# Where the operands of TensorE lie in SBUF: an attention and two MLP layers on one core

## The chip, the core and the metric

The kernel runs on one core of a Trainium2 chip. A core has engines that work side by side, each through its own list of instructions in order: PE (TensorE) multiplies matrices and writes into PSUM, DVE (VectorE), ACT (ScalarE) and POOL (GpSimd) work on elements, and SP issues DMA transfers between HBM and SBUF. An instruction that needs another engine's result waits on a semaphore. SBUF is the memory that the engines read; in each of its 128 partitions a tensor takes a stretch of bytes, and all partitions have it at the same address.

A matrix product on PE has two operands from SBUF. The stationary one (`lhsT`, 128 x 128 here) is loaded into the array by a weight load, which the profile lists apart as PEld; the moving one (`rhs`, 128 x 256 here) then streams through. The load for the next product can run while this one streams.

The metric is the time of one execution on the device, in microseconds (us). Lower is better.

## The reference

The input q, k, v have shape (4, 8, 576, 64): batch, heads, positions, head dimension. The reference computes an attention in two parts, puts the heads side by side, and sends the 2304 x 512 result through two layers with the same formula:

```python
def _attn_ref(q, k, v):
    factor = 4
    # part one: q, k, v averaged over 4 positions, full attention on 144 positions
    out_d = sm_attn(q_d, k_d, v_d)
    out_up = np.repeat(out_d, factor, axis=2)
    # part two: attention over |i - j| < 4 at full resolution
    scores = np.where(mask, scale * q @ k.T, -1e9)
    out_local = softmax(scores) @ v
    return out_up + out_local

x = attn_out.transpose(0, 2, 1, 3).reshape(2304, 512)
x = np.maximum(x @ w_in, 0) ** 2 @ w_out          # w_in 512 x 2048, w_out 2048 x 512
x = np.maximum(x @ w_in2, 0) ** 2 @ w_out2
```

## The kernel before

**The matrix stages.** The tokens are cut into 9 tiles of 256 (`TN`), the 2048 hidden columns into 8 parts of 256 (`NP`). A step is one tile with one part; each layer has 72 steps. To keep fp32 accuracy with PE's faster number format, every operand is split into a high part and a low part (names with H and L, weights with a last digit 0 and 1), and three products are summed: high x high, high x low, low x high.

In a step, `mm_h` (line 802) makes h, 256 hidden columns for 256 tokens: two runs of 12 products, the weight `w{p}0{low}` stationary and the tokens `xH`, `xL` moving, so 24 products. ACT then takes relu and square (lines 813, 815) and writes the high part `gH` (824); DVE makes the low part `gL` (851).

The second product of a step differs by layer. In layer 1, `mm_y` (line 884) makes 24 products with the weight `w{p}1{low}` stationary and `gH`, `gL` moving. In layer 2, `mm_y2` (line 867) uses a scheme with seven block products in place of eight, each in three parts, so 21 products: here pieces of g are stationary (`gH`, `gL`, and `SH`, `gSL`, the high and low part of sums S that DVE makes at line 847, ACT rounds at 830 and DVE subtracts at 856), and the weights are moving. Four of the seven weight blocks are the columns of `w{p}1{low}`; three are sums that are built late in layer 1 and lie in tiles that the attention has given up: they show as q_qk, q_ld, q_xr, q_vw, q_pb, q_qd, q_kd, q_vd, q_outd and q_hd.

**The order of the work.** All instructions are put in order when the kernel is built: small generators for attention groups, weight conversions, splits and products ask a planner (class `Order`) for an engine and a duration, and the planner decides which goes next. PE's order in the dense part is h of step i, then y of step i-1, so that ACT and DVE have one h run to finish g. The planner's costs know nothing of addresses. The attention for all batches, the conversion of the weights from 64-bit numbers (lines 654 to 672) and layer 1 overlap in the first third of the span.

**Where tiles lie.** Tiles of the pool `sb` get addresses in the order in which they are made, each behind the one before. Nearly all are multiples of 1024 or 2048 bytes long per partition, so tiles behind each other have the same address modulo 256 until a shorter one stands between: `nmb` (64 bytes each), `nm` (32 bytes each) and the head tiles (2304 bytes) do that.

Of the kernel before, what the change touches and what calls it, by code (L numbers as in the profile page):

```python
# [8 lines left out]
F32 = mybir.dt.float32  # L9
F32R = mybir.dt.float32r  # L10
# [4 lines left out]
ALU = mybir.AluOpType  # L15
AX = mybir.AxisListType

B, H, S, D = 4, 8, 576, 64
DM, DFF = 512, 2048
GD = S // 4  # L20
TN = 256
# [13 lines left out]
NLD, NGA, NQK, NVW, NPB, NHD = 4, 2, 2, 2, 2, 2  # L35
# [3 lines left out]
XN = [2, 2, 2, 3]  # L39
# [5 lines left out]
CL, GL, HL = 4, 4, 6  # L45
# [161 lines left out]
def attention_two_mlp_kernel(  # L207
# [11 lines left out]
    nc = tc.nc  # L219
    PSUM = bass.MemoryType.PSUM  # L220
    sb = ctx.enter_context(tc.tile_pool(name="sb", bufs=1))
# [8 lines left out]
    def weight(p, kind, low):  # L230

        if (p, kind, low) not in wt:
            wt[p, kind, low] = sb.tile([128, 2 * (2 - kind), 256 * (1 + kind)], F32R, name=f"w{p}{kind}{low}", tag=f"w{p}{kind}{low}")
        return wt[p, kind, low]

    xH = [sb.tile([128, 4, TN], F32R, name=f"xH{i}") for i in range(NXL)]
    gH = [sb.tile([128, 2 * TN], F32R, name=f"gH{i}") for i in range(2)]
    gL = [sb.tile([128, 2 * TN], F32R, name=f"gL{i}") for i in range(2)]
    gSL = sb.tile([128, 512], F32R, name="gSL")
    xL = [sb.tile([128, 4, TN], F32R, name=f"xL{i}") for i in range(NXL)]  # L240
    xr = [sb.tile([128, 4, TN], F32, name=f"xr{i}", tag=f"xr{i}") for i in range(NXR)]
    ld = [sb.tile([128, 512], I64, name=f"ld{i}", tag=f"ld{i}") for i in range(NLD)]
    ga = [sb.tile([128, 512], F32, name=f"ga{i}", tag=f"ga{i}") for i in range(NGA)]
    qk_ = [sb.tile([128, 2, 4, 128], F32, name=f"qk{i}", tag=f"qk{i}") for i in range(NQK)]
    vw_ = [sb.tile([128, 2, 4, D], F32, name=f"vw{i}", tag=f"vw{i}") for i in range(NVW)]
    pb_ = [sb.tile([128, 512], F32, name=f"pb{i}", tag=f"pb{i}") for i in range(NPB)]
    nmb_ = [sb.tile([128, 2, H], F32, name=f"nmb{i}") for i in range(NPB + 2 * XN[0])]
    qd = sb.tile([128, 4, GD], F32, name="qd", tag="qd")
    kd = sb.tile([128, 4, GD], F32, name="kd", tag="kd")
    vd = sb.tile([72, H, 2, D], F32, name="vd", tag="vd")  # L250
    outd = [sb.tile([128, 4, 2 * GD], F32, name=f"outd{i}", tag=f"outd{i}") for i in range(2)]
    hd_ = [sb.tile([72, 4 * GD], F32, name=f"hd{i}", tag=f"hd{i}") for i in range(NHD)]
    nm_ = [sb.tile([72, 2, 4], F32, name=f"nm{i}") for i in range(NHD)]

    spare = {}
    late = [(p, kind, low) for p in range(NP - 1, -1, -1) for kind in (1, 0) for low in (1, 0)]
# [40 lines left out]
    def seven(n, m):  # L297

        t = pair[2 - 2 * (n % 2) if m < 4 else 1]
        return t[:, m % 4 // 2, m % 2 * 256:m % 2 * 256 + 256]  # L300
# [8 lines left out]
    def dve(cols):  # L309
        return "DVE", 0.165 + cols / 960.0  # L310

    def dve2(cols):

        return "DVE", 0.2 + cols / 720.0
# [7 lines left out]
    def act(cols):  # L322
        return "ACT", 0.185 + cols / 1200.0
# [359 lines left out]
    late2 = {}  # L683
# [45 lines left out]
    def quarter(p, name, low):  # L729
        if name in ("T3", "T4", "T2"):  # L730
            w, c = place[p, low][("T3", "T4", "T2").index(name)]
            return w[:, c:c + 256]
        m = ("B11", "T1", "B21", "B22").index(name)
        return weight(p, 1, low)[:, m // 2, m % 2 * 256:m % 2 * 256 + 256]
# [21 lines left out]
    seq = [(layer, t) for layer in (1, 2) for t in range(NT)]  # L756
# [29 lines left out]
    steps = []  # L786
# [21 lines left out]
    def act_h():  # L808
        for i, st in enumerate(steps):
            yield o.at("h", *st)  # L810
            h = hb[i % 2]
            yield act(512)
            nc.scalar.activation(out=h, in_=h, func=AF.Relu)  # L813
            yield act(512)
            nc.scalar.activation(out=h, in_=h, func=AF.Square)  # L815
            if seq[st[0]][0] == 2:
                if seq[steps[i - 1][0]][0] == 2:
                    yield o.at("gl", i - 1)
                if i == last:
                    yield o.at("y", *steps[i - 2])  # L820
                ev["sq", i] = yield act(128)
                nc.scalar.copy(late2["S"][:, 0:128], h[:, 128:256])
            ev["gh", i] = yield act(512)
            nc.scalar.copy(gH[i % 2], h)  # L824
            if seq[st[0]][0] == 2:
                yield o.at("S", i)
                if seq[steps[i - 1][0]][0] == 2:
                    yield o.at("yS", i - 1)
                ev["gsh", i] = yield act(512)
                nc.scalar.copy(late2["SH"], late2["S"])  # L830

    def low_g():
        for i, st in enumerate(steps):
            two = seq[st[0]][0] == 2
            h = hb[i % 2]
            if two:


                yield o.at("sq", i)
                a11, _, a12, a22 = (h[:, 128 * m:128 * m + 128] for m in range(4))  # L840
                s1, s2, s3, s4 = (late2["S"][:, 128 * m:128 * m + 128] for m in range(4))
                for dst, a, b, op in (
                    (s3, a11, s1, ALU.subtract), (s1, s1, a22, ALU.add), (s2, s1, a11, ALU.subtract),
                    (s4, a12, s2, ALU.subtract),
                ):
                    tt = yield dve(128)
                    nc.vector.tensor_tensor(out=dst, in0=a, in1=b, op=op)  # L847
                ev["S", i] = tt
            yield o.at("gh", i)
            tt = yield dve(512)  # L850
            nc.vector.tensor_tensor(out=gL[i % 2], in0=h, in1=gH[i % 2].bitcast(F32), op=ALU.subtract)  # L851
            ev["gla", i] = tt
            if two:
                yield o.at("gsh", i)
                tt = yield dve2(512)
                nc.vector.tensor_tensor(out=gSL, in0=late2["S"], in1=late2["SH"].bitcast(F32), op=ALU.subtract)  # L856
            ev["gl", i] = tt

    def mm_y2(i, first):

        n, p = steps[i]
        some = ((5, 0, "T1"), (6, 1, "T2"), (7, 2, "T3"), (3, 3, "B22")) if first else ((1, 0, "B11"), (2, 2, "B21"), (4, 3, "T4"))
        for m, a, w in some:
            cs = slice(128 * a, 128 * a + 128)
            hi, lo = (late2["SH"][:, cs], gSL[:, cs]) if first else (gH[i % 2][:, cs], gL[i % 2][:, cs])
            for x, (lhsT, low) in enumerate(((hi, 0), (hi, 1), (lo, 0))):
                nc.tensor.matmul(  # L867
                    out=seven(n, m - 1), lhsT=lhsT, rhs=quarter(p, w, low),
                    start=p == 0 and x == 0 and m not in (2, 3, 6),
                    stop=p == NP - 1 and x == 2 and m in (2, 4, 6, 7), skip_group_check=True,  # L870
                )

    def mm_y(i, low):
        n, p = steps[i]
        layer = seq[n][0]
        yb = ybs(n)
        wH, wL = weight(p, 1, 0), weight(p, 1, 1)
        for fi in range(2):
            for w in (wH,) if low else (wH, wL):
                beg = p == 0 and fi == 0 and not low and w is wH  # L880
                end = p == NP - 1 and fi == 1 and low
                g = gL[i % 2] if low else gH[i % 2]
                for e in range(4):
                    nc.tensor.matmul(  # L884
                        out=yb[e // 2][:, (e % 2) * 256:(e % 2) * 256 + 256],
                        lhsT=w[:, fi, e * 128:e * 128 + 128],
                        rhs=g[:, fi * 256:fi * 256 + 256],
                        start=beg and e % 2 == 0,
                        stop=end and e % 2 == 1,
                        skip_group_check=True,  # L890
                    )

    def ybs(n):
        return [pair[1][:, i] for i in range(2)] if n == 1 and LEAD < NP else yb
# [122 lines left out]
    def conversions(layer, t0, dt):  # L1017
        return [
            (t0 + dt * p, convert(layer, p, kind, half)) for p in range(NP) for kind in range(2) for half in range(2)
        ]  # L1020

    o.lane(1, [(-9, act_h())])
    o.lane(1, [(-8, low_g())])
    o.lane(1, [(-7, split_x())])
    o.lane(1, [(-6, leave())])
# [19 lines left out]
    with tc.manual_schedule():  # L1045
# [3 lines left out]
        for n, (c, off, some) in enumerate(((0, 0, (0,)), (0, 3, (1, 2)), (1, 3, (0, 1)), (1, 10, (2,)))):  # L1049
            m = xr[n % 2].rearrange("p k c -> p (k c)")[:, 64 * n:64 * n + 64]  # L1050
            nc.gpsimd.memset(m, 0.0)
            first = off - 64 * c
            nc.gpsimd.affine_select(
                out=m, in_=m, pattern=[[1, 64]], base=3 - first, channel_multiplier=-1,
# [3 lines left out]
                out=m, in_=m, pattern=[[-1, 64]], base=3 + first, channel_multiplier=1,  # L1058
# [35 lines left out]
```

## Time and profile before

| | |
|---|---|
| median of 3 runs | 966.01 us (963.98 to 967.72) |
| span of the profiled execution | 965.6 us |
| PE busy | 925.2 us, 96% |
| DVE busy / ACT busy / POOL busy | 518.5 / 515.6 / 249.8 us |

The profile is of one execution; its own time is the span from the first to the last instruction, 965.6 us, and what lies around it is not in the table. Times in its rows are in us from the span's start. Products on PE overlap each other at their ends, so "busy" of a lone product (0.28 us) is longer than the distance to the next one's start. A distance is found from two starts, or from a merged row of the chain of waits, which counts from the start to the next piece.

### The profile page before, as it was taken

What the parts mean: (1) busy time and instruction counts of PE and PEld (TensorE: products, weight loads), DVE (VectorE), ACT (ScalarE), POOL (GpSimd) and SP (SyncE); (2) the same over time, 40 slices, a digit from 0 to 9 for tenths busy, and PEclk for the clock granted to TensorE, in tenths of its full rate; (3) what the DMA queues carried; (4) which work ended last, traced back from release to release, by engine and by line L of the source; (5) the groups of instructions that cost most, each with busy time, mean ns of one, the idle gap of its engine ahead of it and who ended that gap; (6) DMA issues with size and microseconds to landing.
All of it is one profiled execution on the core that took longest, in us unless ns stands there. A gap on an engine that the chain in (4) does not pass through costs nothing.

```text
span 965.6 us, 21343 instructions
## 1 busy us (share of the span) xinstructions
PE 925.2 (96%) x8778; PEld 885.4 (92%) x8778; DVE 518.5 (54%) x1034; ACT 515.6 (53%) x1045; POOL 249.8 (26%) x228
## 2 busy tenths in 40 slices
PE   7877998989999999999999999999999999999997
PEld 4457988879999999999999999999999999999996
DVE  5599988334444675655321226545454654545454
ACT  4457665545656655545443656545454554545443
POOL 5354557225254210102453454201010110101000
PEclk9799999979999999999999999999999999999999
DMA  8776665236238467565130544011010101100000
GB/s 228 167 197 188 194 188 162 82 114 165 57 104 197 130 200 234 179 209 195 55 102 32 171 134 151 4 44 45 2 44 2 44 1 45 44 2 23 1 23 23
DMA packets 99554, 101.00 MB, mean 105 GB/s; under 512 B 66688, under 2 KB 72320, under 8 KB 99456
## 3 DMA queue, kind: packets, MB, share of 16 engines
q1 hardware_dynamic: 99456, 99.64, 35.0%
q8 instruction: 69, 1.13, 0.5%
q14 instruction: 29, 0.24, 0.1%
HBM read 80.74 MB, written 18.87 MB: 103 GB/s over the span
## 4 chain that ended last, share of the span: by engine, by line
PE 81%; DVE 5%; ACT 2%; issue 1%; POOL 0%; ACTq 0%; DVEq 0%
PE h L802 38%; PE y L884 17%; PE at L867 13%; PE y L867 5%; DVE ga L659 2%; PE at L884 2%; PE at L512 1%; PE at L594 1%; PE at L539 1%; PE at L448 1%; PE at L410 1%; DVE ga L656 1%; PE at L437 1%; PE at L576 1%; DVE S L847 1%
## 5 line engine op out<-in xcount | busy, mean ns | idle before, releaser
L802 PE MATMUL h<-xH,w 128*128 128x256 f32 x2304 | 322.9, 282 | 0.0
L802 PEld LDWEIGHTS h<-xH,w 128*128 128x128 f32 x2304 | 292.1, 189 | 2.4 <-issue 1.4
L813 ACT ACTIVATE h<-h 128x512 f32<-128x512 f32 x144 | 83.9, 582 | 193.3 <-PE h L802 193.2
L802 PE MATMUL h<-xL,w 128*128 128x256 f32 x1152 | 182.4, 280 | 0.0
L851 DVE TENSOR_TENSOR gL<-h,gH 128x512 fp32r<-128x512 f32 x144 | 98.5, 684 | 124.5 <-ACT gH L824 101.0
L802 PEld LDWEIGHTS h<-xL,w 128*128 128x128 f32 x1152 | 156.2, 189 | 0.0
L780 POOL TENSOR_TENSOR xL<-xr,xH 128x512 fp32r<-128x512 f32 x33 | 44.8, 1374 | 346.5 <-ACT xH L329 346.5
L847 DVE TENSOR_TENSOR S<-h,S 128x128 f32<-128x128 f32 x144 | 42.0, 291 | 167.9 <-ACT gH L824 163.7
L884 PE MATMUL y<-gH,w 128*128 128x256 f32 x1024 | 131.7, 280 | 0.2 <-ACT gH L824 0.2
L884 PEld LDWEIGHTS y<-gH,w 128*128 128x128 f32 x1024 | 124.2, 188 | 1.2 <-ACT gH L824 0.6
L659 DVE SCALAR_TENSOR_TENSOR ga<-ld,ga 128x512 int32<-128x512 int32 x128 | 105.2, 823 | 2.7
L830 ACT CAST SH<-S 128x512 fp32r<-128x512 f32 x72 | 44.7, 621 | 90.2 <-DVE S L847 88.1
L815 ACT ACTIVATE h<-h 128x512 f32<-128x512 f32 x144 | 84.1, 584 | 3.4
L824 ACT CAST gH<-h 128x512 fp32r<-128x512 f32 x144 | 84.7, 588 | 2.0 <-DVE S L847 0.5
L884 PE MATMUL y<-gL,w 128*128 128x256 f32 x512 | 72.0, 282 | 0.0
L884 PEld LDWEIGHTS y<-gL,w 128*128 128x128 f32 x512 | 64.3, 188 | 1.1 <-issue 0.8
L856 DVE TENSOR_TENSOR gSL<-S,SH 128x512 fp32r<-128x512 f32 x72 | 54.4, 756 | 10.2 <-ACT SH L830 1.5
L654 ACT ACTIVATE ga<-ld 128x512 f32<-128x512 f32 x64 | 42.5, 670 | 20.6 <-POOL w L668 7.4
L668 POOL TENSOR_TENSOR w<-ga,w 128x512 fp32r<-128x512 f32 x25 | 34.8, 1394 | 54.3 <-ACT w L329 54.3
L656 DVE TENSOR_SCALAR ga<-ga 128x512 int32<-128x512 int32 x64 | 34.9, 545 | 24.8 <-ACT ga L654 24.7
L867 PE MATMUL at<-w,SH 128*128 128x256 f32 x224 | 45.5, 284 | 0.5 <-ACT SH L830 0.5
L847 DVE TENSOR_TENSOR S<-S,h 128x128 f32<-128x128 f32 x144 | 41.3, 287 | 5.3 <-ACT gH L824 0.7
(273 smaller groups left out, 1418.9 us busy)
## 6 DMA issues: line engine op xcount, KB each, us to landing
ld<-in_moe_w_out_dram SPq DMA_DIRECT2D x32, 512.0 KB
ld<-ws SPq DMA_DIRECT2D x24, 512.0 KB
ld<-in_moe_w_in_dram SPq DMA_DIRECT2D x32, 256.0 KB
ld<-in_moe_w_in_dram SPq DMA_DIRECT2D x16, 512.0 KB
ws<-ga SPq DMA_DIRECT2D x32, 256.0 KB
ys<-ld SPq DMA_DIRECT2D x9, 512.0 KB
xr<-ys SPq DMA_DIRECT2D x9, 512.0 KB
vw<-in_v_dram SPq DMA_DIRECT2D x68, 64.0 KB
```

What stands on the lines that cost most here:

```text
L659: nc.vector.scalar_tensor_tensor(out=gi, in0=w32[:, :, word], scalar=amount, in1=gi, op0=op0, op1=ALU.bitwise_or)
L780: engine().tensor_tensor(out=xL[n % NXL][:, ks], in0=xr[i][:, ks], in1=xH[n % NXL][:, ks].bitcast(F32), op=ALU.subtract)
L802: nc.tensor.matmul(out=o, lhsT=w[:, kk, fs], rhs=x[:, kk], start=(i == 0), stop=(i == len(mms) - 1))
L813: nc.scalar.activation(out=h, in_=h, func=AF.Relu)
L815: nc.scalar.activation(out=h, in_=h, func=AF.Square)
L824: nc.scalar.copy(gH[i % 2], h)
L830: nc.scalar.copy(late2["SH"], late2["S"])
L847: nc.vector.tensor_tensor(out=dst, in0=a, in1=b, op=op)
L851: nc.vector.tensor_tensor(out=gL[i % 2], in0=h, in1=gH[i % 2].bitcast(F32), op=ALU.subtract)
L856: nc.vector.tensor_tensor(out=gSL, in0=late2["S"], in1=late2["SH"].bitcast(F32), op=ALU.subtract)
L867: nc.tensor.matmul(out=seven(n, m - 1), lhsT=lhsT, rhs=quarter(p, w, low), start=p == 0 and x == 0 and m not in (2, 3, 6), stop=p == NP - ...
L884: nc.tensor.matmul(out=yb[e // 2][:, (e % 2) * 256:(e % 2) * 256 + 256], lhsT=w[:, fi, e * 128:e * 128 + 128], rhs=g[:, fi * 256:fi * 256 ...
```

## The change

The change moves tiles in SBUF and nothing else. Small tiles (`nmb`, `nm`) and gSL and ga (the latter become S and SH in layer 2) now stand ahead of xH, two pads of 128 and 64 bytes are added, and the four tiles for gH and gL are 128 bytes longer. A function `g_of` picks the place of g inside its tile: at its start or 128 bytes on, by the step's parity and by layer. The built program has the same instructions on each engine in the same order as before.

Addresses modulo 256, as the tile sizes add up in the built program (D is the stationary tile's minus the moving one's, modulo 256; slices of a tile start at multiples of 512 bytes):

| product | stationary | moving | D before | D after |
|---|---|---|---|---|
| h, L802 | w: 192, after 128 | xH, xL: 0, after 64 | 192 | 64 |
| y in layer 1, L884 | w: 192, after 128 | gH, gL: 0, after 64 | 192 | 64 |
| y in layer 2, L867 | gH, gL, SH, gSL: 0, after 192 | w: 192, after 128 | 64 | 64 |
| y in layer 2, L867 | the same | q_qk, q_ld, q_xr, q_vw, q_pb: 0, after 128 | 0 | 64 |
| y in layer 2, L867 | the same | q_qd, q_kd, q_vd, q_outd, q_hd: 128, after 128 | 128 | 64 |

Where a run of one line follows one of another, the load for the new run meets the old run's moving tile. Layer 1: h to y and y to h are 192 before and 64 after. Layer 2: h to y is 0 before and 128 after; y to h depends on the last moving tile (w there is 192 and gives 0, a q_ tile gives 192 or 64) before and 0 after. The attention's tiles keep their places to each other; ident, which its transposes use as the other operand, stays at 128, while ld, qk, vw and pb go from 0 to 128.

```diff
--- before.py
+++ after.py
@@ -233,24 +233,38 @@
             wt[p, kind, low] = sb.tile([128, 2 * (2 - kind), 256 * (1 + kind)], F32R, name=f"w{p}{kind}{low}", tag=f"w{p}{kind}{low}")
         return wt[p, kind, low]
 
+    nmb_ = [sb.tile([128, 2, H], F32, name=f"nmb{i}") for i in range(NPB + 2 * XN[0])]
+    nm_ = [sb.tile([72, 2, 4], F32, name=f"nm{i}") for i in range(NHD)]
+
+
+    def pad(nbytes):
+        sb.tile([128, nbytes // 4], F32, name=f"pad{len(pads)}")
+        pads.append(nbytes)
+
+    pads = []
+    gSL = sb.tile([128, 512], F32R, name="gSL")
+    ga = [sb.tile([128, 512], F32, name=f"ga{i}", tag=f"ga{i}") for i in range(NGA)]
+    pad(128)
     xH = [sb.tile([128, 4, TN], F32R, name=f"xH{i}") for i in range(NXL)]
-    gH = [sb.tile([128, 2 * TN], F32R, name=f"gH{i}") for i in range(2)]
-    gL = [sb.tile([128, 2 * TN], F32R, name=f"gL{i}") for i in range(2)]
-    gSL = sb.tile([128, 512], F32R, name="gSL")
     xL = [sb.tile([128, 4, TN], F32R, name=f"xL{i}") for i in range(NXL)]
+    gHL = [[sb.tile([128, 2 * TN + 32], F32R, name=f"g{c}{i}") for i in range(2)] for c in "HL"]
+
+    def g_of(i, low):
+        two = seq[steps[i][0]][0] == 2
+        c = 32 * ((i + two) % 2)
+        return gHL[low][i % 2][:, c:c + 2 * TN]
+
+    pad(64)
     xr = [sb.tile([128, 4, TN], F32, name=f"xr{i}", tag=f"xr{i}") for i in range(NXR)]
     ld = [sb.tile([128, 512], I64, name=f"ld{i}", tag=f"ld{i}") for i in range(NLD)]
-    ga = [sb.tile([128, 512], F32, name=f"ga{i}", tag=f"ga{i}") for i in range(NGA)]
     qk_ = [sb.tile([128, 2, 4, 128], F32, name=f"qk{i}", tag=f"qk{i}") for i in range(NQK)]
     vw_ = [sb.tile([128, 2, 4, D], F32, name=f"vw{i}", tag=f"vw{i}") for i in range(NVW)]
     pb_ = [sb.tile([128, 512], F32, name=f"pb{i}", tag=f"pb{i}") for i in range(NPB)]
-    nmb_ = [sb.tile([128, 2, H], F32, name=f"nmb{i}") for i in range(NPB + 2 * XN[0])]
     qd = sb.tile([128, 4, GD], F32, name="qd", tag="qd")
     kd = sb.tile([128, 4, GD], F32, name="kd", tag="kd")
     vd = sb.tile([72, H, 2, D], F32, name="vd", tag="vd")
     outd = [sb.tile([128, 4, 2 * GD], F32, name=f"outd{i}", tag=f"outd{i}") for i in range(2)]
     hd_ = [sb.tile([72, 4 * GD], F32, name=f"hd{i}", tag=f"hd{i}") for i in range(NHD)]
-    nm_ = [sb.tile([72, 2, 4], F32, name=f"nm{i}") for i in range(NHD)]
 
     spare = {}
     late = [(p, kind, low) for p in range(NP - 1, -1, -1) for kind in (1, 0) for low in (1, 0)]
@@ -821,7 +835,7 @@
                 ev["sq", i] = yield act(128)
                 nc.scalar.copy(late2["S"][:, 0:128], h[:, 128:256])
             ev["gh", i] = yield act(512)
-            nc.scalar.copy(gH[i % 2], h)
+            nc.scalar.copy(g_of(i, 0), h)
             if seq[st[0]][0] == 2:
                 yield o.at("S", i)
                 if seq[steps[i - 1][0]][0] == 2:
@@ -848,7 +862,7 @@
                 ev["S", i] = tt
             yield o.at("gh", i)
             tt = yield dve(512)
-            nc.vector.tensor_tensor(out=gL[i % 2], in0=h, in1=gH[i % 2].bitcast(F32), op=ALU.subtract)
+            nc.vector.tensor_tensor(out=g_of(i, 1), in0=h, in1=g_of(i, 0).bitcast(F32), op=ALU.subtract)
             ev["gla", i] = tt
             if two:
                 yield o.at("gsh", i)
@@ -862,7 +876,7 @@
         some = ((5, 0, "T1"), (6, 1, "T2"), (7, 2, "T3"), (3, 3, "B22")) if first else ((1, 0, "B11"), (2, 2, "B21"), (4, 3, "T4"))
         for m, a, w in some:
             cs = slice(128 * a, 128 * a + 128)
-            hi, lo = (late2["SH"][:, cs], gSL[:, cs]) if first else (gH[i % 2][:, cs], gL[i % 2][:, cs])
+            hi, lo = (late2["SH"][:, cs], gSL[:, cs]) if first else (g_of(i, 0)[:, cs], g_of(i, 1)[:, cs])
             for x, (lhsT, low) in enumerate(((hi, 0), (hi, 1), (lo, 0))):
                 nc.tensor.matmul(
                     out=seven(n, m - 1), lhsT=lhsT, rhs=quarter(p, w, low),
@@ -879,7 +893,7 @@
             for w in (wH,) if low else (wH, wL):
                 beg = p == 0 and fi == 0 and not low and w is wH
                 end = p == NP - 1 and fi == 1 and low
-                g = gL[i % 2] if low else gH[i % 2]
+                g = g_of(i, 1) if low else g_of(i, 0)
                 for e in range(4):
                     nc.tensor.matmul(
                         out=yb[e // 2][:, (e % 2) * 256:(e % 2) * 256 + 256],
```

## Rows read from the trace of the kernel before

**Rows 1.** The page: busy us, share, instructions; the granted clock in 40 slices.
```profile
PE 925.2 (96%) x8778; PEld 885.4 (92%) x8778; DVE 518.5 (54%) x1034; ACT 515.6 (53%) x1045; POOL 249.8 (26%) x228
...
PEclk9799999979999999999999999999999999999999
```
**Rows 2.** The page: the chain that ended last, by engine and by line.
```profile
PE 81%; DVE 5%; ACT 2%; issue 1%; POOL 0%; ACTq 0%; DVEq 0%
PE h L802 38%; PE y L884 17%; PE at L867 13%; PE y L867 5%; DVE ga L659 2%; PE at L884 2%; PE at L512 1%; PE at L594 1%; PE at L539 1%; PE at L448 1%; PE at L410 1%; DVE ga L656 1%; PE at L437 1%; PE at L576 1%; DVE S L847 1%
```
**Rows 3.** Stretches: us, then PE, PEld, DVE, ACT, POOL busy, clock, DMA.
```profile
0.00:147.00 147.00, 120.62 (x1185) 96.63 (x1185) 118.27 (x187) 87.52 (x179) 73.76 (x75) 0.94 0.73 194
147.00:330.00 183.00, 177.38 (x2035) 165.92 (x2036) 88.04 (x171) 103.42 (x255) 73.09 (x71) 0.96 0.46 124
330.00:580.00 250.00, 250.00 (x2371) 247.64 (x2370) 110.83 (x187) 126.61 (x227) 70.53 (x64) 1.00 0.47 151
```
**Rows 4.** The chain of waits, 300 to 640 us: start, length, what.
```profile
373.84 2.83 PE y L884 x24
...
450.81 2.72 PE y L884 x24
453.53 2.72 PE h L802 x24
...
489.48 2.83 PE y L884 x24
```
**Rows 5.** The timeline of PE in a step of layer 2: start, length, line, tiles.
```profile
718.56 1.10 PE L802 MATMUL h<-xH,w 128*128 128x256 f32 x8
...
719.97 0.40 PE L867 MATMUL at<-w,SH 128*128 128x256 f32 x2
720.21 0.28 PE L867 MATMUL at<-w,gSL 128*128 128x256 f32 x1
720.32 0.28 PE L867 MATMUL at<-q_outd,SH 128*128 128x256 f32 x1
...
721.04 0.40 PE L867 MATMUL y<-w,SH 128*128 128x256 f32 x2
...
721.39 0.39 PE L867 MATMUL y<-w,gH 128*128 128x256 f32 x2
...
722.07 0.28 PE L867 MATMUL y<-q_outd,gH 128*128 128x256 f32 x1
```
**Rows 6.** The timeline of PE in a step before that.
```profile
710.78 0.40 PE L867 MATMUL at<-q_qk,SH 128*128 128x256 f32 x2
...
711.50 0.40 PE L867 MATMUL y<-w,SH 128*128 128x256 f32 x2
```
**Rows 7.** The chain of waits in layer 2.
```profile
674.92 2.83 PE h L802 x24
677.75 2.46 PE at L867 x21
```
**Rows 8.** Stretches, by line: the first three L802, the other two L884.
```profile
147.00:330.00 183.00, 68.62 (x504) 0.96 0.46 124
330.00:580.00 250.00, 125.45 (x1008) 1.00 0.47 151
580.00:965.60 385.60, 209.03 (x1680) 1.00 0.09 31
...
147.00:330.00 183.00, 67.93 (x504) 0.96 0.46 124
330.00:580.00 250.00, 125.55 (x1008) 1.00 0.47 151
```
**Rows 9.** Timelines of ACT and DVE in the step of rows 5.
```profile
714.88 0.58 ACT L813 ACTIVATE h<-h 128x512 f32<-128x512 f32 x1 [1.25 <-PE h L802]
...
718.89 0.69 DVE L856 TENSOR_TENSOR gSL<-S,SH 128x512 fp32r<-128x512 f32 x1
```
**Rows 10.** Waits, 560 to 640 us: total, times, longest.
```profile
PEld at L867 <- DVE gSL L856: 1.5, 3, 0.8
```

## The prediction

> **What bounds the kernel now.** I read four views, in this order. First the page's busy table: PE is busy 96% of the span, and its granted clock is at its upper level in nearly every slice [rows 1]. The chain that ended last says the same by engine and line: 81% of the span is PE, and the lines of the two matrix stages (h at L802, y at L884 and L867) carry almost all of that [rows 2]. Then the table by stretch: up to 147 us PE is busy 120.62 of 147 us beside a DVE that is busy 118.27; from 147 to 330 us PE is busy 177.38 of 183; from 330 us on it does not pause [rows 3]. Up to 147 us the chain runs over DVE lines (L659, L656) more than over PE, so there a faster PE is worth little; behind it, time is the number of matmuls times the distance from one start to the next.
>
> That distance is the number the change is about, and the busy column hides it, since a lone matmul is shown as 0.28 us long while the next starts after 0.11 to 0.12. So I take distances from starts. Call D the address of the stationary operand that is loaded next minus the address of the moving operand that streams now, modulo 256 (the table in the section on the change).
>
> - L802 and L884 have D = 192 throughout. The chain shows 24 of them in 2.83 us, 117.9 ns each, at 373 and 489 us; but the same lines, tiles and addresses take 2.72 us, 113.3 ns each, at 450 us [rows 4]. So this work has two holds at one clock, and 113.3 is reached without any change of the work.
> - In the second layer the y products (L867) have the stationary g at 0 in every row and three kinds of moving tile. With moving "w" (at 192, so D = 64) a run of six starts at 721.39 and the next group at 722.07: 0.68 us, 113.3 ns each, step after step. With moving q_outd and q_vd (D = 128) the six from 720.32 end at 721.04: 0.72 us, 120 ns [rows 5]. With q_qk (D = 0) six take 711.50 - 710.78 = 0.72 us as well [rows 6].
> - The h run between, D = 192 again, takes 719.97 - 718.56 = 1.41 us for 12, 117.5 ns [rows 5], and 2.83 for 24 in every step [rows 7].
>
> Same instruction, same shape, same clock: the distance follows the pair of addresses. At D = 64 it goes to the short hold from whatever came before, within about three matmuls: the first three "w" products after an h run take 720.32 - 719.97 = 0.35 us against 0.34 at the short hold, so a switch costs about 0.01 us [rows 5]. At D = 192 the long hold is the usual one, and the short one was met by luck.
>
> [...]
>
> **The change part by part.** No instruction is added, removed or moved on any queue, DMAs and waits included; only SBUF places differ. After it D is 64 for every pair inside an h run, an L884 run and an L867 run; what is left are two switches in each step of layer 2 (h to y: 128, y to h: 0). Lines L802, L884 and L867 are taken in four stretches, counts from [rows 8]:
>
> - Up to 147 us: 0. DVE sets the chain there. If a quarter of it came through it would be about 0.5 us.
> - 147 to 330 us: 504 + 504 matmuls. All of them at 4.5 ns less (117.8 - 113.3) would be 4.5 us; but PE idles 5.6 us there, a part waits on other engines, and a part already runs at the short hold. Between 0 and 4.5 I take 2.2.
> - 330 to 580 us: 1008 + 1008. Between 437 and 481 us they are at the short hold already: 44 / 0.1133 = 388. The other 1628 x 4.5 ns = 7.3 us.
> - 580 us to the end: 1680 h x 4.5 ns = 7.6 us. The y products, 21 in a step, take 2.46 us [rows 7], 117.1 each; 21 x 113.3 = 2.38, and with two switches 2.40, so 0.06 less in 72 steps = 4.3; rows of other steps show 2.43 to 2.46, so I take 3.6.
>
> Sum: 2.2 + 7.3 + 7.6 + 3.6 = 20.7 us.
>
> **What is late next.** In layer 2 each step has a loop that PE does not set: from the end of h, ACT (start 714.88) and DVE follow, and gSL is done at 718.89 + 0.69 = 719.58 [rows 9]; its first reader is the third product of the run that starts at 719.97, at 720.21 [rows 5]. The slack is 0.63 us less what the load needs ahead (about 0.1). A step that is 0.17 us shorter leaves about 0.35, so this loop doesn't become the bound. It is short only where DVE is held up, in the first steps of layer 2, where the weight load already waits 1.5 us in 3 places for gSL [rows 10]: there a faster PE only waits longer. Some four such steps at 0.17 give back 0.7 us. DVE, ACT and POOL read and write moved tiles too. No row ties their durations to a place; I take 0 and, from the 0.7 us of one DVE instruction here or there on the chain, half a us either way. The attention's own matmuls keep their relation (qk with qk, pb with vw), except that the transposes' input moves from 128 off ident to 0 off; those two offsets run at the same 0.72 us for six.
>
> So 20.7 - 0.7 = 20.0 us less: 965.6 - 20.0 = 945.6 for the span. The profiled execution's span is 0.4 us under the median of the three timed runs, 966.0, so I set 0.4 around it: **946.0 us**.
>
> The ends: everything at the short hold without switches and the whole of 147 to 330 us: 4.5 + 7.3 + 7.6 + 5.1 + 0.5 = 25, so 941. At the other end the long hold stays in part (first rival), 955, and with less of 147 to 330 us and a further us lost behind gSL, 958; I stop at 960.
>
> **Rivals.**
> 1. *D = 64 has two holds as well.* For it: D = 192 shows both, and the L867 rows at D = 64 are never longer than nine in a row, while h runs have 24. Against it: all those runs settle, every step. If half of the h and L884 stretches stayed at 117.8: 1.1 + 3.7 + 3.8 + 3.6 - 0.4 = 11.8 less, 954.
> 2. *Not the difference decides but the moving operand's own place* (slower). All L867 rows have stationary at 0, so they don't part "64 above" from "moving at 192". If a moving tile at 192 is quick and one at 128 slow, as q_outd is [rows 5], then after the change every L867 product streams from 128 at 120 ns, not 117.1: 1512 x 2.9 ns = +4.4. h and L884 stream from 64, which no row shows; at 120 ns also they would add (1628 + 1680) x 2.2 ns = 7.3, and the 388 lucky ones 6.7 ns each, 2.6. That is 970 to 980, most likely 972. It decides as soon as a run of 24 h takes over 2.83 us. Against it: D = 192 shows that moving at 0 can run at 113.3 [rows 4], so the moving place alone doesn't fix the distance.
> [...]
>
> **How the numbers follow.** Forecast 0.70; rival 1 0.12; rival 3 0.10; rival 2 0.08. What a measurement of this kernel can tell from no change is about 0.5%, so faster means under 961.2 and slower over 970.8. Faster: 0.70 + 0.12 + a little of the edge = 0.83. Same: 0.10. Slower: 0.07, since part of rival 2 stays below 970.8. The range 941 to 960 holds the forecast's own 941 to 951 and rival 1, about 0.8.
>
> **What would show it.** Right: the chain of waits has 24 h and 24 L884 products at 2.72 us everywhere behind 330 us, also directly after a stall, and 21 L867 products at about 2.40, with q_ tiles no longer apart from w; a layer-2 step of about 5.12 us in place of 5.29; busy time of DVE and ACT unchanged. [...]

## The result, and the profile after

The changed kernel takes 956.9 us (median of 4 runs, 955.97 to 958.01) against 966.4 us in the same comparison: a ratio of 0.990 (95% interval 0.9886 to 0.9921). That is faster, clear of the noise, but 9.5 us were gained where 20 were forecast (946). The profiled execution has a span of 954.2 us, where before had 965.6.

On the page PE is as full as before [rows 1] and its granted clock shows the same tenths in nearly every slice; only its busy time is shorter. Columns as in rows 1:

```profile
PE 914.5 (96%) x8778; PEld 874.8 (92%) x8778; DVE 518.2 (54%) x1034; ACT 515.1 (54%) x1045; POOL 249.1 (26%) x228
...
PEclk9889999979999999999999999999999999999999
```

The chain of waits from 300 to 640 us answers to [rows 4] (line 816 is h now, 898 the y of layer 1):

```profile
320.60 2.83 PE y L898 x24
...
354.85 2.83 PE y L898 x24
357.68 2.83 PE h L816 x24
360.50 2.83 PE y L898 x24
363.77 2.74 PE h L816 x24
366.50 2.72 PE y L898 x24
...
550.60 2.72 PE y L898 x24
```

From 366 us to the end of layer 1 all h and y runs reach the short hold, as forecast; nearly all take 2.72, and a few directly behind attention products or with a pause inside take up to 0.3 us more. But at 320 and 354 to 363 us runs of 24 stand at 2.83, with D = 64 as in all the others. Before had 2.72 at the first of these places:

```profile
321.91 2.72 PE y L884 x24
```

So D = 64 has the long hold too.

Layer 2 in the chain of waits, which answers to [rows 7] (line 881 is the y of layer 2):

```profile
671.94 2.74 PE h L816 x24
674.68 2.47 PE at L881 x21
677.15 2.74 PE h L816 x24
679.89 2.47 PE at L881 x21
```

And the timeline of PE in one step there, which answers to [rows 5]:

```profile
716.77 0.40 PE L881 MATMUL at<-q_xr,SH 128*128 128x256 f32 x2
...
717.47 0.40 PE L881 MATMUL y<-w,SH 128*128 128x256 f32 x2
...
717.83 0.40 PE L881 MATMUL y<-w,gH 128*128 128x256 f32 x2
...
718.53 0.28 PE L881 MATMUL y<-q_vd,gH 128*128 128x256 f32 x1
```

h fell from 2.83 to 2.74. The 21 y products did not fall: 2.47 against 2.46. The q_ products lost their own, slower distance (six from 716.77 to 717.47 take 0.70 us, where before had 0.72), but the w products lost their short one: six from 717.83 to 718.53 take 0.70 us, 117 ns each, where before had 113.3 at the same D = 64. What else could have changed did not: DVE and ACT are as busy as before, and the waits for gSL in the first steps of layer 2 ([rows 10]: 1.5 us, 3 times) are as long as they were:

```profile
PEld at L881 <- DVE gSL L870: 1.6, 3, 0.8
```

A ledger by work, not by time, shows where the gain lies. In each trace I take the start of the first h or y product behind the 480th, behind the 1488th and behind the 3440th (about 148, 330 and 572 us before), and the end.

| stretch | before | changed | forecast | measured |
|---|---|---|---|---|
| to the 480th product | 147.8 | 146.1 | 0 | -1.7 |
| 480th to 1488th | 182.4 | 182.8 | -2.2 | +0.4 |
| 1488th to 3440th (rest of layer 1) | 242.0 | 236.0 | -7.3 | -6.0 |
| 3440th to the end (layer 2) | 393.4 | 389.3 | -10.5 | -4.1 |
| span | 965.6 | 954.2 | -20.0 | -11.4 |

The first row belongs to the start: there the chain runs over DVE in both, and it moves by some us from execution to execution (the first h product began between 66.1 and 74.4 us in the traces below). Without it 9.7 us are gained, which is what the medians say (9.5). A second profile of the changed kernel (e6_changed below) has 181.4, 236.0 and 389.4 in the other three rows: the second row moves by 1.4 us from execution to execution, the last two by 0.2 at most.

### The profile page after: what moved, and what is told of

It is laid out like the page before. It is cut to its first block, busy times and chain, and to the rows that moved or that the text cites. A ratio compares the mean times of both kernels' runs of the same rounds, so it can differ in the third digit from the quotient of the medians.

```text
span 954.2 us, 21343 instructions
## 1 busy us (share of the span) xinstructions
PE 914.5 (96%) x8778; PEld 874.8 (92%) x8778; DVE 518.2 (54%) x1034; ACT 515.1 (54%) x1045; POOL 249.1 (26%) x228
## 4 chain that ended last, share of the span: by engine, by line
PE 81%; DVE 5%; ACT 2%; issue 1%; POOL 0%; ACTq 0%; DVEq 0%
PE h L816 38%; PE y L898 17%; PE at L881 13%; PE y L881 5%; DVE ga L673 2%; PE at L898 2%; PE at L526 1%; PE at L608 1%; PE at L553 1%; PE at L462 1%; PE at L424 1%; DVE ga L670 1%; PE at L451 1%; PE at L590 1%; DVE S L861 1%
## 5 line engine op out<-in xcount | busy, mean ns | idle before, releaser
L816 PE MATMUL h<-xH,w 128*128 128x256 f32 x2304 | 318.0, 281 | 0.0
L816 PEld LDWEIGHTS h<-xH,w 128*128 128x128 f32 x2304 | 288.3, 190 | 2.4 <-issue 1.3
L816 PE MATMUL h<-xL,w 128*128 128x256 f32 x1152 | 179.3, 278 | 0.0
L816 PEld LDWEIGHTS h<-xL,w 128*128 128x128 f32 x1152 | 153.5, 189 | 0.0
L898 PE MATMUL y<-gH,w 128*128 128x256 f32 x1024 | 129.6, 280 | 0.2 <-ACT gH L838 0.2
```

What stands on the lines that cost most here:

```text
L816: nc.tensor.matmul(out=o, lhsT=w[:, kk, fs], rhs=x[:, kk], start=(i == 0), stop=(i == len(mms) - 1))
L898: nc.tensor.matmul(out=yb[e // 2][:, (e % 2) * 256:(e % 2) * 256 + 256], lhsT=w[:, fi, e * 128:e * 128 + 128], rhs=g[:, fi * 256:fi * 256 ...
```

## The experiments

Call E the D of a switch: the address of the first stationary tile of a run minus that of the last moving tile of the run before. The entry theory, from the traces above: D = 64 has two holds, 113.3 and 117.8 ns, and E together with the hold before picks one. The place theory (rival 2): the moving tile's own address decides. The hold of a run is given as the mean of its last 16 distances from start to start in m1 and m2.

### The holds by themselves (m1_holds)

A kernel of PE runs with no work on other engines beside them, so that no other engine's traffic can pick the hold. `run(bank, stationary, moving, n)` issues n products; places count in steps of 32 bytes, `k` is 64 bytes, and the tiles lie at all multiples of 32. Each block has these three lines (loops left out, comments put in):

```python
run(2, base, base + k, 4)            # kick
run(1, base + k, base, RUN)          # ref: D = 64, entered with 0
run(0, base + enter, base + enter - d, RUN)   # test: entered with E, at D
```

> A kernel of PE runs alone; it leaves the whole computation of the reference out. Each block is 4 products that set the entry, a reference run of 24 with D = 64 entered with D = 0, and a test run of 24 whose first load has entry offset E against the reference's moving tile and whose products have offset D; E and D take the 8 multiples of 32, and all is done twice, the second time 64 bytes further. Entry theory (D = 64 has two holds, 113.3 and 117.8 ns from start to start, and a run keeps the one that its entry gives): the reference runs, all entered with D = 0, take 24 x 113.3 = 2.72 us after the first few products; the test runs at D = 64 take 2.72 when entered with 0 or 64 and 2.83 when entered with 128; both halves agree. Place theory (the moving tile's own place decides, 64 and 192 short, 0 and 128 long): reference runs take 2.83 with the moving tile at 0 in the first half and 2.72 with it at 64 in the second, whatever the entry. [...]

The chain of waits shows the blocks in turn. Here base 0 and E = 0; the tests have D = 0, 32, 64, 96, 128, 160 and 192:

```profile
18.42 2.83 PE ref L31 x24
21.25 2.88 PE test L31 x24
...
27.43 2.84 PE test L31 x24
...
33.56 2.74 PE test L31 x24
...
36.77 2.73 PE ref L31 x24
39.50 2.82 PE test L31 x24
...
45.62 2.85 PE test L31 x24
...
51.67 2.87 PE test L31 x24
...
57.75 2.72 PE test L31 x24
```

The block with E = 128 and D = 64, with base 0 and with base 64:

```profile
225.13 2.74 PE ref L31 x24
227.87 2.83 PE test L31 x24
...
614.19 2.73 PE ref L31 x24
616.92 2.83 PE test L31 x24
```

Of the 8 values of D only 64 and 192 reached 113.3 ns; the others stayed between 116.6 and 120.2, whatever E. At D = 64, E = 0, 32, 160 and 224 gave 113.3, and 64, 96, 128 and 192 gave 117.8; at D = 192 only E = 0 gave 113.3. The two halves, 64 bytes apart, gave the same hold in all 64 pairs of tests and all 64 pairs of reference runs. That ends the place theory. Placement is not without effect either: test runs that differ in their addresses alone take from 2.72 to 2.88 us. My own first form of the entry theory failed too: reference runs, all entered with 0, were long in some blocks (2.83 us at 18.42) and short in others (2.73 at 36.77). What came before counts as well.

### All places moved by 64 bytes (e1_shift64)

```diff
     pads = []
+    pad(64)
     gSL = sb.tile([128, 512], F32R, name="gSL")
```

> The changed kernel with everything from gSL on 64 bytes further, so that each D stays and only the places differ (x and the g of layer 1 at 128, w and q_ at 192, the g of layer 2 at 0). Entry theory: as the changed kernel, 957 +- 2 us, 24 h in a layer-2 step 2.74 us, 21 y products 2.47. Place theory: 24 h go back to 2.83 and 24 L898 products too (moving at 128), the 21 y products fall to 2.39 (moving at 192): layer 1 loses 6 us, layer 2 stays, 963.

958.1 us, ratio to before 0.9906 (0.9874 to 0.9938): as the changed kernel. Layer 2 in the chain of waits has the same lengths to the last digit:

```profile
690.55 2.74 PE h L817 x24
693.29 2.47 PE at L882 x21
```

### The switches exchanged (e2_d128)

Slots for the weights are made first, those of w_out together, with a pad behind them; the pads ahead of the other tiles are set so that D is 64 in every run (these lines of the diff are left out here).

```diff
+    for kind in (1, 0):
+        for p in range(NP):
+            for low in range(2):
+                sb.tile([128, 1024], F32, name=f"slot{p}{kind}{low}", tag=f"w{p}{kind}{low}")
+        if kind:
+            pad(128)
```

> As the changed kernel, but the out-weights and the q_ tiles lie 128 bytes from the in-weights modulo 256; every D inside a run is 64 still, and the switches change: layer 2 has h to y 0 and y to h 128 (changed kernel: 128 and 0), layer 1 has 192 both ways (changed: 64). Entry theory: the two layer-2 runs swap their holds: 21 y products 2.39 us and 24 h 2.83; 5.22 a step, so layer 2 as in the changed kernel; layer 1 not foretold, between 2.72 and 2.83 for 24; 955 to 965 us. Place theory: h streams from 192 (short, 2.72), y of layer 2 from 128 (long, 2.47): as the changed kernel, 957.

960.4 us, ratio 0.9931 (0.9907 to 0.9956). In layer 2 the two kinds of run have changed places, as the entry theory says and the place theory does not. Layer 1 has 192 both ways; of its runs of 24 behind 330 us without a stall inside, h is long in 30 of 34 and y short in 28 of 34. Layer 2:

```profile
690.60 2.40 PE at L888 x21
693.00 2.83 PE h L823 x24
```

### No switch in layer 2 (e3_dm64)

The same edit with `pad(64)` and other pads ahead, so that w_out lies 64 below w_in.

> As the changed kernel, but the out-weights and the q_ tiles lie 64 bytes below the in-weights modulo 256; every D inside a run is 64 still, and layer 2 has 64 at both switches as well, so no switch is felt there; layer 1 has h to y 0 and y to h 128. Entry theory: in layer 1 the y products are short (24 in 2.73) and h long (2.83), so 330 to 580 us loses about 3 us against the changed kernel; layer 2 keeps one hold through whole stretches between stalls: 5.10 us a step if short (8 us less than the changed kernel over 72 steps) or 5.30 if long (6 us more). 951 to 966 us. Place theory: h streams from 64 and the y of layer 2 from 64, both short in every step, 5.10; the y of layer 1 from 0, long; 952.

961.4 us, ratio 0.993 (0.9905 to 0.9955). Layer 1 came as foretold: counted as in e2, y is short in 32 of 34 runs (2.74) and h long in all 34 (2.83). Layer 2 keeps one hold through whole tiles and changes it only in a run that has a stall inside, three times: to short at 596 us, to long at 623, and to short again at 794 (nine products in 1.14 us at 794.40, where 1.06 or 1.02 is usual). Other stalls, up to 0.9 us long, left the hold as it was. Addresses are the same throughout; nothing differs but what came before:

```profile
620.39 2.72 PE h L825 x24
...
625.89 2.83 PE h L825 x24
...
788.04 2.47 PE at L890 x21
790.51 2.83 PE h L825 x24
793.34 1.06 PE y L890 x9
794.40 1.14 PE at L890 x9
795.54 0.34 PE y L890 x3
795.88 2.72 PE h L825 x24
798.60 1.02 PE at L890 x9
799.62 1.36 PE y L890 x12
```

From 795.88 a step takes 2.72 + 1.02 + 1.36 = 5.10 us, against 2.83 + 2.47 = 5.30 in the long hold: the whole price of the hold in layer 2 is 0.2 us x 72 = 14 us.

### Every switch between runs at D = 64 (m2_switches)

Two kinds of run in turn, switches E and 128 - E (loops left out, comments put in):

```python
run(1, k, 0, RUN)                    # ref
run(0, enter, enter - k, RUN)        # test
```

> A kernel of PE runs alone; it leaves the whole computation of the reference out. Part one: runs of 24 that all have D = 64, two kinds in turn, with switch E to the second kind and 128 - E back, E in the 8 multiples of 32, ten pairs each, once without stalls and once with PE stalled by ACT before every second pair. Entry theory, with what the first such kernel showed (from the short hold, 160 and 224 stay short, 96, 128 and 192 turn long; from the long hold, 0 and 32 turn short): E = 160 has switches 160 and 224 and stays at 113.3 in nearly all its runs, also after stalls; E = 224 has 224 and 160 and does the same; E = 0 and 128 alternate, one kind short and one long; E = 64 keeps one hold until a stall. A theory by which the holds come by chance: about as many long as short runs for every E. Part two: D in steps of 16; where a hold of 113.3 exists only at 64 and 192, all others stay at 116.5 to 120.

The chain of waits where E = 128 (and 0 back) gives way to E = 160 (and 224 back), at 297.62 us:

```profile
292.05 2.74 PE ref L35 x24
294.79 2.83 PE test L35 x24
297.62 2.75 PE ref L35 x24
300.37 2.72 PE test L35 x24
303.09 2.74 PE ref L35 x24
```

The part without stalls gives this table for runs at D = 64 (short: a hold under 115 ns; the first run of each E, which follows another E, is left out):

| hold before | switch to short | switch to long |
|---|---|---|
| long | 0 (19 of 19), 32 (10), 96 (10), 192 (9) | 64 (19), 128 (1) |
| short | 160 (19 of 19), 224 (19) | 32 (9), 96 (9), 128 (18), 192 (10) |

So 0, 32, 96, 128 and 192 bring no lasting hold: two kinds of run take turns, as h and y do in the changed kernel (128 and 0). 64 keeps what it finds. 160 and 224 stay short, in 40 of 40 runs without stalls and in 40 of 40 with a stall before every second pair. That they put a long run right is not shown by this: none of these 80 runs was long, and a stall seldom leaves a long one (at the other E, 25 of the 30 runs directly behind a stall are short too). From long through 160 there is one run, in part two, and it is short; from long through 224 there is none. In part two, D in steps of 16, the short hold came at 64, and with one of the two entries at 240 (113.3) and nearly at 144 (114.4), which I had not foretold; at 192 both entries stayed at 117.8.

### Every switch at 160 or 224 (e4_d96)

The edit of e2 with `pad(160)` behind the w_out slots and other pads ahead: w_out lies 96 bytes above w_in, modulo 256. Then layer 1 has 160 and 224, layer 2 has 224 and 160, and D is 64 in every run.

> As the changed kernel, but the out-weights and the q_ tiles lie 96 bytes above the in-weights modulo 256: every D inside a run is 64, the switches are 160 and 224 in layer 1 and 224 and 160 in layer 2. Entry theory: both kinds of run settle at the short hold in both layers: 24 h 2.73, 24 y of layer 1 2.73, 21 y of layer 2 2.40; a layer-2 step 5.13 us in place of 5.21, 6 us over 72 steps, and 1 to 3 us more in layer 1 where the changed kernel has long stretches up to 365 us: 949 us (946 to 952). If a switch of 160 or 224 does not put a long run right: as the other kernels with switches that alternate, 957 to 961.

954.5 us (952.0 to 958.1), ratio 0.9868 (0.9847 to 0.9889). The profiled execution, 952.0 us, has a span of 950.2. Layer 2 in the chain of waits has both kinds short:

```profile
681.84 2.72 PE h L824 x24
684.57 2.40 PE at L889 x21
686.97 2.72 PE h L824 x24
```

A step is 5.13 us, as expected, but the time is not: 954.5 lies above the 946 to 952 that I gave. By the ledger the stretches are 147.5, 181.2, 236.9 and 384.6 us. Layer 2 is 8.8 us under before and 4.7 under the changed kernel, where 6 were expected; the steps with stalls gave the rest back. Layer 1 is no better than in the changed kernel, where 1 to 3 us were expected: the two switches of a step cost some 0.02 us together (2.74 and 2.72 for its runs), and a run that stays at 64 pays none (2.72 for both in the changed kernel behind 366 us).

What becomes of a long run shows in layer 2 of the second profile of this layout (e7_d96 below). Behind a y run that a stall left long, the run of h entered with 160 is long too, and the y run behind it, entered with 224, is short again:

```profile
708.72 0.36 PE y L889 x3
709.08 2.83 PE h L824 x24
711.90 1.04 PE at L889 x9
712.94 1.37 PE y L889 x12
714.31 2.72 PE h L824 x24
```

In both profiles together, counting runs without a stall behind a run at about 118 ns: through 224 all 11 came out short, through 160 only 3 of 14 did. So it is 224 that puts a long run right; 160 mostly keeps it.

### One part alone (e5_x_only)

```diff
+    sb.tile([128, 32], F32, name="pad0")
     xH = [sb.tile([128, 4, TN], F32R, name=f"xH{i}") for i in range(NXL)]
+    xL = [sb.tile([128, 4, TN], F32R, name=f"xL{i}") for i in range(NXL)]
+    sb.tile([128, 32], F32, name="pad1")
     gH = [sb.tile([128, 2 * TN], F32R, name=f"gH{i}") for i in range(2)]
     gL = [sb.tile([128, 2 * TN], F32R, name=f"gL{i}") for i in range(2)]
     gSL = sb.tile([128, 512], F32R, name="gSL")
-    xL = [sb.tile([128, 4, TN], F32R, name=f"xL{i}") for i in range(NXL)]
```

> The kernel before with the token tiles xH and xL alone moved, by 128: h has D = 64 as in the changed kernel, the y of layer 1 keeps 192, the y of layer 2 keeps 64 on w, 0 and 128 on q_ tiles. One part of the change alone. Difference theory (D sets which holds there are, the switch which is met): h gets short runs in layer 1 in part, since the switch from y is 192 there, and in layer 2 in part; the w products of layer 2, entered with 128 now and not with 0, are long at their start; 958 to 965. If all the gain came from h at D = 64 whatever is around it, 24 h at 2.72 to 2.74 everywhere and 957 at most; if h alone changes nothing, 966.

964.8 us, ratio 0.9965 (0.9953 to 0.9977). h is at D = 64 here and still short only in part: counting runs of 24 without a stall inside at a mean under 115.3 ns, 17 of 34 behind 330 us in layer 1 and 40 of 71 in layer 2. The y of layer 1, at D = 192, is long in all 34. So D = 64 inside the h runs is not enough; the runs around them have a part in it, as expected.

### The two layouts side by side (e6_changed, e7_d96)

No edit: the changed kernel and that of e4, on one chip beside the same runs of before.

> The changed kernel again, on the same chip and beside the same runs of the kernel before as the next one, so that the two can be set against each other. Entry theory: a layer-2 step 5.21 us, 24 h 2.74, 21 y 2.47; 0.990 of the kernel before.

> The kernel with switches of 160 and 224 again, beside the changed kernel. Entry theory: a layer-2 step 5.13 to 5.17 us, all of the difference in the 21 y products (2.40 against 2.47); 3 to 6 us less than the changed kernel, all of it in layer 2, layer 1 equal within 1 us; 0.986 of the kernel before. If the 4 us between the two profiles came from the chip and not from the places: equal.

957.2 us (ratio to before 0.9893, 0.9875 to 0.991) and 953.7 us (0.9865, 0.9842 to 0.9888). The medians are 3.5 us apart in the expected direction, the intervals overlap a little. The profiles are clearer: the 600 h and y products behind the 4500th take 70.0 us in e6 and 69.9 in the first profile of the changed kernel, 69.1 and 69.0 in the two of the other layout, 70.7 before. The whole of layer 2 by the ledger is 389.4 and 389.3 us against 384.9 and 384.6. (The whole span of e7's profile, 957.0, is longer because its first h product came at 74.4 us, not at 66.6.) So the layout of e4 beats before for certain, and it beats the changed kernel in layer 2.

## Why the prediction was wrong

- **What bounds the kernel, and what D does: right.** The gain came from the distances of L802 and L884 products on a full PE (24 in 2.72 to 2.74 us for 2.83); no other engine took the place, the waits for gSL did not grow (1.6 us for 1.5), and the slower distances of D = 0 and 128 are gone (six in 0.70 us for 0.72).
- **The step that failed** is "At D = 64 it goes to the short hold from whatever came before, within about three matmuls". It has a long hold that lasts (e3, 24 in 2.83 us), and a switch of 128 out of a short run leads into it (m2, 18 of 18). In the rows of before every w run that I had read was entered with 0 from a long h run, or followed q_ products. 128 stood there only out of a q_ product at 120 ns (q_outd to w at 721.04 in [rows 5]), and behind that the run did turn short; out of a short run, as the change makes it, 128 stood in no row. I noted that h to y would be 128, and counted it as 0.01 us.
- **Its price.** The y products of layer 2 were to fall by 3.6 us and did not (2.47 for 2.46 us). h fell to 2.74 and not to 2.72, since a switch of 0 costs its first products 116 to 122 ns: 0.084 x 72 = 6.0 for 7.6. The 4.1 us of layer 2 are these 6.0, less 1.0 for the y products (0.014 x 72) and about 0.9 in the steps with stalls. From the 480th to the 1488th product 2.2 were forecast, and between nothing and 1.0 came (the two profiles of the changed kernel): between attention products and stalls, runs fall into either hold, as at 320 and 354 us. The rest of layer 1 gave 6.0 of 7.3.
- **Rival 1** had the mechanism, two holds at D = 64, at 0.12 and 954 us. What picks between them it left open; the switches do (e2, m2). That 956.9 comes near its 954 is partly luck: it counted on 3.6 us from the y products, which did not come, and had half of the other h and y work stay long, of which nearly all turned short behind 366 us.
- **Rivals 2 and 3.** Rival 2 ended with m1 and e1. Rival 3, no change at 966 us, ended with the measured gain of 9.5 us; a stall still has a part in the hold, since at switches of 64 it changed only in runs with a stall inside (layer 2 of e3, three times).
- **The rows that should have warned me** are [rows 4] themselves: 2.83 and 2.72 at one D, changing at a stall (at 436.7 us, with two distances of 162 and 223 ns, and at 480.5 us, with 268 and 227). I took that for a property of D = 192 instead of asking what had led there. Why D = 192 shows both is still open: in m1 it reached 113.3 only where it was entered with 0, and in m2 not there either (117.8).
- **The term of 0.7 us** for DVE in the first steps of layer 2 cannot be told apart from the rest.

## What to carry to other kernels

Where PE is full and nothing waits, read the distance from start to start by pairs of operands: here products of one shape stood at 113.3 and at 117.8 ns by where the two operands lay and what ran before, and that was worth 1% (966.4 to 956.9 us) without moving an instruction. The D inside a run is half of it: with h alone moved to D = 64, 40 of 71 h runs in layer 2 were short (e5), and a switch of 128 turned 18 of 18 short runs long (m2). So lay out the switches as well, and prefer a pair that came back to the short hold after a stall (here 160 and 224: 5.13 us a step of layer 2 in e4) over one that kept what it found (64: 5.10 or 5.30 us in e3). When one trace shows the same work at two speeds, find out what picks between them before forecasting that a change will.

## What was not expected of the hardware

In the traces of these runs a stream of products, 128 x 128 stationary and 128 x 256 moving, has two lasting distances at one set of addresses, 113.3 and 117.8 ns. At switches of 64 it kept either: in layer 2 of e3 all changes lie at three of the stalls. The picture repeated after 64 bytes of common shift (m1: the same hold in all 64 pairs; e1: 2.74 and 2.47 us, as in the changed kernel). It went with the offset, taken modulo 256, of the next stationary tile from the present moving one: in m1, at D = 64, E = 0, 32, 160 and 224 gave 113.3 ns and the other four 117.8. What inside the chip makes this pattern is not shown by these runs; nor is why 224 mends a long run (11 of 11 in e4 and e7) and leaves a short one (19 of 19 in m2), while 32 and 96 mend a long one (10 of 10 each in m2) and spoil a short one (9 of 9 each).
